# Four K and Q loads issued by ScalarE, and new lists for the first units of a sparse-attention and MLP kernel

## The chip, the cores and the metric

The kernel runs on one core of a Trainium2 chip. The core has five engines that work side by side, each on its own list of instructions: TensorE (PE; its weight loads are shown as PEld), VectorE (DVE), ScalarE (ACT), GpSimd (POOL) and SyncE (SP). In this kernel SP issues DMAs only. The metric is the time of one execution on the device in microseconds (us).

## The reference, cut to what matters

Four batches of eight heads, 768 positions, head size 64. For every query the six best of 24 chunks of 32 keys are chosen by an upper bound from each chunk's smallest and largest key; attention runs over these chunks with a causal mask; the result, with the heads side by side, goes through an MLP with an ELU.

```python
k_min, k_max = k_chunks.min(3), k_chunks.max(3)          # chunks of 32 keys
ub = sum(maximum(q * k_min, q * k_max))                  # per query and chunk
ub = where(causal, ub, -1e9)
top_chunks = argsort(ub)[..., -6:]
scores = where(sel & (pos_q >= pos_k), q @ k.T / 8, -1e9)
x = softmax(scores) @ v                                  # [3072, 512], heads side by side
h = x @ w_in                                             # 512 -> 2048
out = where(h > 0, h, exp(min(h, 0)) - 1) @ w_out        # 2048 -> 512
```

## The kernel before

The work is cut into eight units of 384 query rows. Units 0 and 1 are made of 192 positions each of batches 0 and 1: unit 0 ("p") has positions 0 to 191, where every query takes all of its chunks, and unit 1 ("s") has positions 192 to 383, where chunks are chosen. Units 2 to 7 are half a batch each. For each unit the attention of its rows is followed by an MLP of 16 tiles of 128 hidden channels. Attention of one unit and the MLP of an earlier one are woven into each other.

Names of operations, as the text uses them (b is the batch, u the letter p or s, G a group of four heads, r a pair of heads, x a block of 96 rows):

- `ldk..`, `ldq..`, `ldv..` load K, Q, V into buffers `f` (11 of them, 128 x 512 f32): `ldq1s00` is Q of batch 1, unit s, block 0, and `ldq1s10` block 1. `ec...` copies chunk rows into `lhs`. `wq..` loads Q of unit p on POOL, with a cast to bf16.
- `kT`, `qT` (lines 423 and 408): K and Q are transposed on TensorE into a PSUM bank; `kt`, `qt`, `qh` copy that out, `ka`, `qa` put it into the operands of the score matmuls, `qr` is a relu of Q, `kmin`, `kmax`, `ks` are the chunk bounds.
- `tr` (mask, line 705), `sc` (scores), `ex` (exponential, on ScalarE), `pv` (P times V, line 775), `rcp` and `on` (division, lines 657 and 667 on VectorE or 664 on ScalarE), `px` and `xt` (transposes of the result and their copies).
- `v0p0` and the like convert V to bf16. `ub` (line 613) are the bound matmuls of the choice, `ubT`, `max`, `lt`, `sT`, `mk` make its mask.
- The MLP of unit i: `h0.5` is tile 5 of unit 0 (four matmuls of line 872 into a bank); `e0.5` (ScalarE, exponential), `m0.5` (POOL or VectorE) and `g0.5` (VectorE) make the ELU and free the bank. `o0.1.2` is row tile 1, quarter 2 of the second matrix (line 896).
- `w_in1` (tiles 4 to 7), `w_in0` (0 to 3), `w_in2` (8 to 15) and `w_out0` to `w_out3` load the weights on POOL, with a cast.
- `fill` is a matmul on zeros, 22 of them at the start.

Nothing is scheduled while the kernel runs. A string `ORDER` has three characters for each operation: the engine and the operation's number. A string `PLACES` gives the slot of each buffer (a PSUM bank, an `f` buffer and so on) in order of first use. Each engine works strictly through its own operations in the order of that string; an operation waits until what it reads is there and until the slot that it writes has been left by its earlier buffer's readers.

```python
for j in range(0, len(order), 3):
    o = g.ops[64 * DIGITS.index(order[j + 1]) + DIGITS.index(order[j + 2])]
    for b in o.bufs:
        if b.slot is None and b.cls != "fixed":
            b.slot = DIGITS.index(next(places))
    o.emit({"P": PE, "A": ACT, "D": DVE, "G": POOL, "S": SP}[order[j]])
```

The functions that the change touches:

Of the kernel before, what the change touches and what calls it, by code (L numbers as in the profile page):

```python
# [38 lines left out]
ORDER = """
G0vS0UD00D01PjXA02D09PjYS0sPjZG0wD06Pj-D0iPj+S0uPk0G0aPk1D0oS0rPk2A0TD0jG0kPk3A0tPk4S0XD03G04Pk5  # L40
Pk6Pk7Pk8D05G0bP1mD0lG0cG0WP1hP1nPk9S2dG0eG0pG0VPkaPkbPkcP0KA0OD0PPkdPkeG0nG0gG0fS2fPkfPkgD0qD0m
P18P0RP0IG0dD0SD0MP0BS0zA0JA1cP0+P1iD0CS0xA0FD19P1oP1jS0ZD10D1aD13S2eD0LS2gA1qA1pA15D11GmCP16P1f
P1sS2MA1lGmBD0ND0DD0GS2PS2tP1xA1gD17G0AG08G0yP1wA1kD12P1rP1yS2ND0QP1tA1AGmDP1VA1vA1zD0-P1BP1CP1W
D1DP24P23D25A1uG0YP27P28D26G07D1EG1eP1PP1GD29P1QP1-D1XA2aG0EP1ZD1+D20P1MP1FP1LG2hD1HP2bG1bG2QD1R
P2zD1IA1YP2mD2AP1JD2nP2HP21S2GD1ND1OA1SP1TA2qD2oS2OA1KD22P2uD1UA2cPmYG0HG2sA2ID2BG0hD2pG2CPn4AmZ
Dm-Dm+Pn0An5PmUGn6An1D2vA2JGmEPmQD2wAmVDbqP3jDn7Gn2Dn3A2DS2RAmRGmWPn8A2rG14D3lA1dPmIG2xAn9D3kD3m
GmFA2yPmMD3nPngGnaDmXAmNGmSDnbAmJPnEA2KGmODmTPnsPnAAnhGmGD3oA2FAnFGmKDniPnkD3pGmHDmPA3qA3sPnoDnj
G3rAntP3FDmLAnpGnGPncA3GGnuDnHPnOAnBGnqDnvAndGnCS2kDnrAnlP3+PnwGneA40DnDS2iP3HDnfP36D38A3IP2VD37
P3ZA3tG2LP4jPnIA3-D2XD2WA2ZS4ZPnPA2EG39GnmA2+G2YP4BA3aDnnPnVA4CD41A4kP4DA4EP31P4hP3ePnJA3fD32D33
A4iAnxGnyD4FPnQD34D3gP3uG3JG35DnzG3cG3bPnWA2SD3wS3dA2-D3vD3yD3xA3iS30PnXPnYD3zD2lS2TG2jD3AA3BPnR  # L50
S4-PnKS4YAnSD3ES4XP3LD3CP4MA3hD4lD3DA4NP42DnZP46S4VP3KP43P4GP48A47P4HG2UP4KA49D4IP3QD4JPnLS4WA4L
D3MD3NG4aA3RD4OP3OP4nP4sS7SP4cD44P4bAnMA4tP4mD45P4qA3PD4dD4eP5pP4PP5OS7PA4rG4uD3SP4QD4oP4fP3TA5P
P3UD4RD4SS4+P5dA4gD3VP4TD3WG5RA5qP4wP4vD4pA5eP5CP3XSaLD5QD4xD4yP56A5DS55P5iD57A5aS7QP4zP5HD3YA4A
P5vG7TD4UA5ED58PoHG5gS51Sn-A5mPo3AoID5wA5LPovD5kGoJAo4D5JG59PojA5GG5sD5zA5rPo7Go5DoKAokD5IG5KD5j
PobAowAo8D5xG5lPofA5MGolDo6PoPGo9DomAocA5fS53D7RPoDGodAoQDoaG5yS7UPonA5hGoxDoeAoEGoRPn+SnNDoyAoo
GoFAogScXDoSPozGopA5BDoGPorS8jAo0GohDoqS7LP5TGo1DoiAosA5FDo2S7MGotA5SG5NDouA5tPoLG5bD5VAoAPo+A50
G7VD5UAoMD5XGoBPp0A5oGoNA5cD5WPpcPpdD5YD5ZPp5SnUS5uDoCPp6A5-G5+SaFDoOPpeD61A54DaMP64P6eA65DaOP62
P6aP6gA63Pp1A6bD60A6hDaNP6kP66A6fP6jP68D5nP6cDaPA6lPp7A67G6mD52A6dP6zSaQP6vPoTA69D6iS7KA6AP6tA6w
P6oSnTA6uP6FP6nAoUS7WP6xA6GPoXD6pGoVS7ND6qA6yG5AP6HDoWAoYP6rP6KGbkP6LS7OScPD6sA6IP79GoZP7aP74A6M
P6YDo-PpfA75D6JA7bD6NShDScVG7cDaRP6DA6ZPp2ApgA6EP6BA6CP70P6-P76P6PDp3A6+A77DaSP6ODaTA71P7AP72A73  # L60
P6WA6XP7vP7xA7wA7yDaUP7XD78D6QSb1P6UA6VPp8Ap9P7BSphSp4G7zP8eA8fD7YD7+D6RD7ZP7pP7jP7dP7eP7rP87P7n
D8gA7CG7DD7fD7gD88D89G8iG8hP7tP8wD8xA7kA7qA7oA7sP7lA7mA7uP8kP6SP8DP7EScQSaADb2A8AD8BG8CA6TA8bG8d
P7FD7GD7HA8oP7hA7iP82A83P8rA8sAaGA8tD8mP7ID7JPpiPpCPpOPpqPpKD8yD8pD8cG8aG7-G80SazSaEApDApPDb3D8z
DaWD8lD8EGpEDpFAcWGpQDpRDbmG8nG8qA84A8FDd3ApLDpMDpNPpGPpyApjGpkDplAprP8ID8KD8JScSSaBSaCSpbSaHShF
ApHApzA8HAbnG85GpsG8uD8MDptGpIDpJA81AcYGd0GpADpBPqaAqbPpuPpmApnGpoDppDc+ApvGpwDpxAbpD8LPpSApTDpU
PpWPqeApXGqcD8NA86GpYDpZPq2Pp-Pq6PqiPqjPquPqvD8OScZGc-AbjAaIAq3Ap+Aq7DpVGq0Dq1Dq4Dq5DqdA8PP8TP98
PqkGq8Dq9Ad2AqfGqgDqhSboSaJGaKA8UP99A8GA9aD9bP95A96P8VA8WPqwP8XA8YP91A92P93A94P8ZA8-PqxP8+A90D8R
D8SDaVD8QP9iP9mPakP9wD8vGaXA9jA9xSaDPbxP9uAbyDqyPqlA9vAalD97P9dP9cP9qP9sP9zP9kSfpScRGd5ScTSflSd1
ScUDqmA9nA9tP9AA9BGhID9yD9eD9fA9lA9rP9VA9WPqoD9CPaYP9gD9hP9oA9pP9NPbCA9OP9DPamAanP9PP9-P9EP9+A9Q
# [34 lines left out]
010234561723809400a15670000116732123410154351712367920340512011326120372504022630201740451602060
0001712105100321222310106020041302422105371001210657208104429601a202b10225c63d5074344173e0675174
232002354f0131811a051702149562710202334657702101110353224400271111415003200024301667235013082223
6211124241g0321703025031511642080210211a14023024060172b50d501200217001e9903040645563645270036705
340231510610a143324462420c4518036175460720352160242050221360512703003437015067105025412256406301
2015462720241f034232126300182750369851002011b24115422110702d5117600120301271a12022e1g1502921a044
5364106150341652360311745073a7480420141216521017436560746000200310074351642530340701436007410610  # L110
42322012500347220410676023221c798035120b001246202d1701400505612260110022020f000241743012305621e0
071112221931755412a2640316137544050011601a47135720640203353013120721001117220g041122026531002711
74c02263021d1670105693482300e122f61101154501822304b674310511676271325701101360217051295706272306
123706204523075601020103360271112010022300042411320a621132020237250411ce0252361030170751421bg120
20612350204814010012f010001652733027095310264575302140352735620410026321622347203011031211521200
6712400d341281052302217b02012a13620c211102507243023ef7110g61154420673450256564172631401101225514
60750413270731412054725631203017020025041190221232010711c1006140dg1135221041b7200210711e220f6451
1532608172011
# [51 lines left out]
def kernel(  # L170
# [134 lines left out]
    def dma(dst_src, writes, reads, name, engines=(SP,)):  # L305
        def emit(e):
            d, s_ = dst_src()
            eng[e].dma_start(out=d, in_=s_)
# [693 lines left out]
```

## Time and profile before

| | |
|---|---|
| median of 3 runs | 281.22 us (280.7 to 281.28) |
| profiled execution, its own time | 281.2 us |
| its span, first to last instruction | 279.5 us |
| mean granted TensorE clock | 0.980 |
| busy: PE, DVE, ACT, POOL | 96%, 78%, 78%, 46% of the span |
| DMA | 38.07 MB, mean 136 GB/s; 95,136 of 103,747 packets under 512 B |
| queues | q1 (issued by SP) 32.75 MB, q0 (by POOL) 4.59 MB, q10 (by ACT) 0.30 MB |

The span is cut in tenths and slices on the page; times in the text are microseconds from the span's start. A busy TensorE is not TensorE at its peak: a matmul's time in the groups overlaps its neighbours', so lengths are read from runs of matmuls in the chain. A DMA issue has two times: how long it holds the issuing engine's list, and how long until the data have landed.

### The profile page before, as it was taken

The numbers are of one execution on the slowest core, as the hardware profiler recorded it, in microseconds if no ns is written. First come the engines' busy times: TensorE is split into PE (matmuls) and PEld (weight loads), VectorE is DVE, ScalarE is ACT, GpSimd is POOL, SyncE is SP. The second block draws the span as 40 slices with busy tenths as digits, with TensorE's granted clock in tenths as the row PEclk, the third lists the DMA queues.
The fourth block names the chain that finished last, engine by engine and source line by source line (L and its number), as shares of the span: only waits on it lengthen the run. The fifth ranks groups of instructions, "written<-read, shape, count | busy, mean of one in ns | idle before, by whom it ended". The sixth has DMA issues, their size and how long they took to land.

```text
span 279.5 us, 6962 instructions
## 1 busy us (share of the span) xinstructions
PE 267.7 (96%) x2458; PEld 165.3 (59%) x2458; DVE 217.2 (78%) x655; ACT 217.0 (78%) x491; POOL 128.1 (46%) x256
## 2 busy tenths in 40 slices
...
GB/s 147 211 195 210 224 197 185 216 237 248 53 59 220 233 236 196 211 150 111 192 169 114 116 218 224 69 41 135 164 4 1 58 39 4 14 126 90 20 11 101
DMA packets 103747, 38.07 MB, mean 136 GB/s; under 512 B 95136, under 2 KB 99488, under 8 KB 103712
## 3 DMA queue, kind: packets, MB, share of 16 engines
q1 hardware_dynamic: 95696, 32.75, 55.4%
q0 software_dynamic: 6832, 4.59, 10.9%
q10 hardware_dynamic: 1184, 0.30, 0.5%
...
q14 instruction: 16, 0.13, 0.2%
...
## 4 chain that ended last, share of the span: by engine, by line
PE 75%; DVE 8%; ACT 5%; POOL 2%; issue 2%; DMA 1%; DVEq 0%; ACTq 0%; POOLq 0%
PE bank L896 25%; PE bank L872 24%; PE bank L803 10%; PE bank L854 5%; PE bank L613 3%; PE bank L564 2%; DVE gT L885 2%; ACT pt L818 1%; POOL m L881 1%; PE bank L914 1%; PE bank L690 1%; PE bank L423 1%; ACT e L879 1%; PE bank L775 1%; PE bank L749 1%
## 5 line engine op out<-in xcount | busy, mean ns | idle before, releaser
L872 PE MATMUL bank<-xt,w_in_sb 128*128 128x384 bf16 x512 | 90.2, 328 | 0.3 <-DMA xt<-on 0.2
L896 PE MATMUL bank<-w_out_sb,gT 128*128 128x512 bf16 x368 | 89.3, 379 | 0.0
L881 POOL TENSOR_SCALAR m<-e 128x384 f32<-128x384 f32 x100 | 52.0, 529 | 62.0 <-ACT e L879 51.5
L885 DVE SCALAR_TENSOR_TENSOR gT<-bank,m 128x384 bf16<-128x384 f32 x128 | 65.7, 549 | 9.7 <-POOL m L881 8.4
L879 ACT ACTIVATE e<-bank 128x384 f32<-128x384 f32 x128 | 59.1, 493 | 16.0 <-PE bank L872 13.0
L872 PEld LDWEIGHTS <-w_in_sb 128*128 128x128 bf16 x512 | 49.7, 98 | 35.5 <-issue 4.6
L818 ACT ACTIVATE pt<-bank 128x384 bf16<-128x384 f32 (+1 forms) x144 | 67.1, 547 | 3.6 <-PE bank L803 2.5
L896 PEld LDWEIGHTS <-gT 128*128 128x128 bf16 x368 | 34.6, 97 | 36.1 <-issue 2.2
L803 PE MATMUL bank<-rhs,lhs 96*128 96x384 bf16 (+2 forms) x240 | 42.8, 293 | 1.0 <-DVE on L667 0.5
L835 POOL TENSOR_TENSOR pt<-pt,tri 128x256 bf16<-128x256 bf16 (+1 forms) x18 | 16.4, 916 | 38.5 <-ACT pt L822 23.9
L803 PEld LDWEIGHTS <-lhs 96*128 96x128 bf16 x240 | 21.7, 97 | 13.9 <-issue 0.9
L854 PEld LDWEIGHTS <-pt 128*128 128x128 bf16 x576 | 21.0, 97 | 3.6 <-ACT pt L818 0.2
L854 PE MATMUL bank<-vext,pt 128*128 128x65 bf16 x576 | 22.1, 193 | 0.0
L667 DVE TENSOR_TENSOR on<-bank,rcp 128x384 bf16<-128x384 f32 (+1 forms) x37 | 18.7, 510 | 1.3
L326 POOL CAST rhs<-qt 64x384 bf16<-64x384 f32 x24 | 12.8, 539 | 11.8 <-ACT qt L324 10.8
L324 ACT ACTIVATE o<-bank 128x512 f32<-128x512 f32 (+1 forms) x14 | 8.1, 588 | 13.0 <-PE bank L896 10.1
L657 DVE RECIPROCAL rcp<-bank 128x6 f32<-128x6 f32 (+1 forms) x40 | 7.2, 185 | 13.5 <-PE bank L854 9.0
L371 DVE TENSOR_REDUCE kst<-bank 128x12 f32<-128x384 f32 x32 | 16.5, 548 | 1.3 <-ACT kt L324 0.7
L326 DVE COPY o<-bank 128x512 f32<-128x512 f32 (+1 forms) x11 | 7.2, 665 | 12.2 <-PE bank L896 10.0
L835 DVE TENSOR_TENSOR pt<-pt,tri 128x512 bf16<-128x512 bf16 (+1 forms) x30 | 11.2, 390 | 5.4 <-ACT pt L822 3.6
L324 ACT ACTIVATE rhs<-qt 64x384 bf16<-64x384 f32 x28 | 14.2, 518 | 0.5
L822 ACT ACTIVATE pt<-bank 128x512 bf16<-128x512 f32 x24 | 14.0, 604 | 0.7 <-PE bank L803 0.4
...
## 6 DMA issues: line engine op xcount, KB each, us to landing
...
```

The lines of the kernel that those rows point to most:

```text
L324: nc.scalar.activation(out=dst, in_=src, func=AF.Copy)
L326: eng[e].tensor_copy(out=dst, in_=src)
L667: nc.vector.tensor_tensor(out=ap(on)[:, 0:nt].rearrange("p q h d -> p h q d"), in0=view()[:, :, :, 0:D], in1=ap(rcp)[:, :, 0:nt].to_broadc ...
L803: nc.tensor.matmul(ap(banks[hd])[:, o + pc:o + pc + wd], lhsT=apl(ls, G)[0:96, pr, hd, P * kb:P * (kb + 1)], rhs=ap(rs)[0:96, hd, c0 - HS ...
L818: lambda e, hd=hd, pt=pt, banks=banks, wtot=wtot: nc.scalar.activation(out=ap(pt)[:, hd, PAD:PAD + wtot], in_=ap(banks[hd])[:, 0:wtot], fu ...
L835: eng[e].tensor_tensor(out=view, in0=view, in1=tri[:, 64:64 + P].rearrange("p (a b w) -> p a b w", a=1, b=1) .to_broadcast([P, 2, len(dg), ...
L854: nc.tensor.matmul(view()[:, hd, qi, :], lhsT=ap(pt)[:, hd, P * qi + off:P * qi + off + P], rhs=ap(vx[b])[:, kb, 2 * r + hd, :], start=(kb ...
L872: nc.tensor.matmul(ap(bank)[:, 0:HS], lhsT=w_in_sb[:, kk, P * fc:P * (fc + 1)], rhs=ap(xT[i, kk]), start=(kk == 0), stop=(kk == NKK - 1))
L879: g.op(f"e{i}.{fc}", (ACT,), lambda e, eb=eb, bank=bank: nc.scalar.activation(out=ap(eb), in_=ap(bank)[:, 0:HS], func=AF.Exp), reads=[(ban ...
L881: g.op(f"m{i}.{fc}", (POOL, DVE), lambda e, eb=eb, mb=mb: eng[e].tensor_scalar(out=ap(mb), in0=ap(eb), scalar1=-1.0, scalar2=1.0, op0=AOT. ...
L885: nc.vector.scalar_tensor_tensor(out=ap(gt), in0=ap(bank)[:, 0:HS], scalar=0.0, in1=ap(mb), op0=AOT.max, op1=AOT.min),
L896: nc.tensor.matmul(ap(bank), lhsT=ap(gts[fc])[:, P * tt:P * (tt + 1)], rhs=w_out_sb[:, fc, :], start=(fc == 0), stop=(fc == NFC - 1))
```

## The change

The code changes in one place: the loads of K and Q of batch 1, unit s, may be issued by ScalarE.

```diff
-                            (SP, ACT) if u == 0 and n == "k" else (SP,))
+                            (SP, ACT) if (u, n) == (0, "k") or (b, u) == (1, 1) else (SP,))
```

The rest of the diff is in the two strings. Read back into names, SP's list after its first eleven issues, which are the same, and ScalarE's to the first MLP exponentials:

```diff
 SP
  ... ldk0s10 ldq0s10
- ldk1s00 ldq1s10 ec000 ldk1s10 ec001 ldq1s00 ldv1s0 ldv0s1 ldv0s0 ldq011 ec101 ec100 ldv1s1
+ ec000 ec001 ldv1s0 ldv0s1 ldv0s0 ldq011 ec101 ec100 ldv1s1
  ldq012 ldq010 ldk012 ldk010 ldk011 ldv111 ldq112 ...
 ACT
  table ldk1p00 ldk0p10 kt0p1
- qh0p0 kt1p1 kt0p0 ex0p11 ex0p10 ka11p0 ex0p01 qh1p1 ex0p00 ex1p11 ex1p01 ex1p10 ex1p00
- on1p3 on0p2 on1p1 kt0s0 xtp0 xtp3 qt0s1 e0.4 e0.6 e0.5 qr0s1 e0.3 kt0s1 e0.2 ka00s0 ka01p1
+ ka00p1 ka10p1 qh0p1 ex0p11 kt1p0 ex0p00 ex0p10 ex0p01 qh1p1 qh1p0 ka11p1 ex1p10 ex1p11 ex1p00 ex1p01
+ ka10p0 on0p2 ldk1s00 ldk1s10 on1p1 ldq1s10 xtp0 xtp3 kt0s0 ldq1s00 e0.5 qt0s0 ka01p1 e0.6 e0.4 ka00s0
 DVE
- rcp0p0 rcp0p3 on0p3 on0p0 rcp1p3 rcp0p2 rcp1p2 on1p2 rcp1p0 rcp1p1 on1p0
+ kmax0p0 v0p0 rcp0p3 on0p3 rcp0p0 on0p0 rcp0p2 rcp1p3 on1p3 rcp1p0 rcp1p2 on1p2 on1p0 rcp1p1 rcp0p1
 POOL
- oh es1 es0 w_in1 w_in0 v0p1 tris2 v0p0 w_in2 v1p0 tris1 ka11p1 ks0p0 vc0 ks1p1 vc1 ka10p0 ka10s0 kq ks0s1 m0.6 w_out0
+ oh ks0p1 ka00p0 w_in1 v1p0 es0 w_in0 v0p1 ka01p0 v1p1 w_in2 kq ka11p0 ks0p0 vc1 es1 ka10s0 w_out0 ks0s0 m0.6
 PE (MLP of unit 0 and the scores of unit s)
- h0.4 h0.6 h0.5 h0.3 h0.2 ub00 h0.7 h0.0 h0.1 h0.9 h0.15 h0.12 h0.14 h0.10 h0.11 sc0s00 h0.8 o0.1.0 sc0s11 h0.13 sc0s01 kT1s1 kT1s0 ... o0.0.0 o0.1.1 ... qT1s0 sc0s20 qT1s1
+ h0.5 h0.6 h0.3 h0.2 h0.4 ub00 h0.0 h0.7 h0.1 h0.15 h0.11 h0.9 kT1s1 h0.12 h0.14 h0.8 sc0s10 sc0s00 h0.10 sc0s01 h0.13 kT1s0 o0.0.0 sc0s11 sc0s31 o0.2.0 qT1s1 o0.1.0 sc0s30 o0.1.1 qT1s0
```

Besides, identb goes from VectorE to POOL, the memsets rz and vz0 from POOL to VectorE, v0p0 from POOL to VectorE, on1p3 from ScalarE to VectorE, qt0s0 from VectorE to ScalarE, qt0s1 the other way, and some thirty other small operations of the units p and s change engine or place. Of the 22 fills 18 instead of 14 stand at the very start. The engines' own lists from about 108 us on are the same. The slots of the buffers follow the new order. No operation is added and none is left out.

More of the change, by code (lines that the diff above doesn't have):

```diff
@@ L39 @@
 ORDER = """
[L40 to L66, printed above, removed]
+G0vS0UD00D01PjXA02D09PjYS0sPjZG0wD06Pj-D0iPj+S0uPk0Pk1D0oS0rPk2A0TD0mD0jG08G0aG07G0eG0kPk3A0tPk4
+S0XD03G04G0bG0cPk5Pk6Pk7Pk8Pk9PkaPkbPkcP18PkdPkePkfP0KPkgG05A0OP0BP1iP1mP1nP0RD0pD19D1cA0PD0MD0n
@@ new lines @@
+D1aD0LD0FG0WS2dG0VS2fG0gA0QP0ID0JP0+D10D11D0lP1xA0SP1oP1hP1jS0zA1qA13S0xS0ZA1kD0CD0qD0DG0NG0GS2e
+S2gGmCG0YG0dGmBS2tP1sP1rA1pA1lP1fA1gP16A17P1wP1yA1eA1zP1tA1AA1uA1vG0AD0yP24P23P1MD25P1WP1CD26P1B
+D1DD1EP1VD1XG14G0-P28P27D29P1FP1-P1LP1ZP1GP1PP1QD2aP2bGmDA0HA1YD1HD1+D20A2MP2HP21D1ID1RP2zP1JP2m
+A2NA1SA2PD1ND22D1bD1OP1TD2IP2uD2hD2JD1UA1KA2cPn0A2qA2OS2GD2oAn1Pn4G0hG15D2AD2nD2BA2vD2wDbqA1dPmU
+PmQPmYG0EG2QG0fG2sGmEG2pD2CP3jAn5Gn6Dn7AmZDm-A2rAmRGn2G2LG2xDn3Dm+D3lD3kS2RGmSDmTAmVGmWDmXD3nD3m
+PmIAmJGmKDmLD3oPn8An9GnaPmMAmNA2KGmODmPD3pD2yGmFG12PnEPnoAnpPngA2DAnhDniGmGGmHP36GnqDnbDnrDnjG3r
@@ new lines @@
+A3qAnFGnGDnHPnsAntGnuDnvS2kA2FPnAPncAndP3ZA3-AnBP3FPnkA3GGneD38A3sD2EDnCDnDDnfP3HD3aG3cA3tPnwP2V
+PnIP3+A3IS2iD37A2ZS4ZP4DPnVP3eA40AnlDnmA2-A4EAnxDnnD2XD2WD2YG3bGnyPnOP4BA3fA4CG2SPnPG2+P31D32D3g
+A34P4jP4hA4iA3iPnJA4kA3hPnWPnXD2lD33D39P3uS3dS30PnQPnKDnzPnRAnSD3wD3yD3vD3xD3zD3AD3CA3EA3BS2TPnY
+DnZS4-S4YS4XG41G4FG35G2jP43G3JG4lP3KP4GP4KP48A49P46A47S4VP3LP4MD3MG2UP42D44P4HD45D4IA4NA4LS4WP3Q
+PnLA3RAnMP3OG3DP4qP4sG4aP4bS7SD4OD3ND4JP4cP4QD4dD4eA3PD3SA4rA4tG4uP4nP5pP4PS7PP4mP4fP5OP3UP3TP5d
+A5qA5PG5RD4RD4oD4SP4TS4+A4gP4vP4wP5CP56D3VD3WP3XSaLA5eA4pD5QA5DP5iD4xD4yP4zA4AS55S7QP5HP5vD4UD3Y
@@ new lines @@
+D57G5gA5mA5EPoHAoIS51Sn-Po3A5LA5aPojPovAo4D58G59G7TGoJA5GG5sD5wD5IA5rPo7Go5D5JDoKD5kAokD5jG5KPob
+AowAo8D5xD5zG5lA5MGolDo6PoDPoPGo9DomAocA5fS53D7RGodAoEAoQDoaG5yS7UPofPonA5hGoxDoeGoRPn+SnNDoyAoo
+GoFAogScXDoSGopA5BDoGPorPozS8jAo0GohDoqS7LGo1DoiAosA5FDo2S7MGotA5SDouA5tPoLG5bP5TD5VAoAA50G5NG7V
+D5UAoMD5XGoBPo+Pp0A5oGoNA5cD5WPpcD5YD5ZPp5Pp6SnUS5uDoCA5-G61G5+SaFD52DaMDoOPpdPpeA54P64A65DaOP62
+A63P6gP6aA6bP6ePp1D60A6hDaNP6jP6kP66A6fD5nDaPA6lG6mP68P6cA69A67A6dP6zA6APp7P6vP6tPoTD6iP6oSnTS7K
+S7NSaQA6wP6FP6nA6uAoUS7WP6xA6GPoXD6pD6qA6yG5AP6HGoVDoWAoYP6rP6LP6KGbkS7OScPD6sA6IP79P7aP74A6MP6Y
@@ new lines @@
+GoZDo-PpfA75A7bA6ZD6ND6JShDScVG7cDaRDaTP6DP6BP70P6-Pp2A6EApgA6CP76P6PDp3A6+A77DaSP6OA71P7AP72A73
+P6WA6XP7vA7wP7xA7yDaUP7XD78Sp4Sb1P6UA6VPp8Ap9P7pSphG7zP8eP7BA8fD7YD7+D6QD6RD7ZP7jP7dP7eP7rP7nD8g
+A7CG7DD7fD7gP87D88G8iG8hP7lP8wD8xD89A7kA7sA7qA7oA7mP8kP7tA7uP6SP8DP7EScQSaADb2A8AD8BG8CA6TA8bG8d
+P7FD7GD7HA8oP7hA7iP82A83P8rA8sAaGA8tD8mP7ID7JPpiPpCPpOPpqPpKD8yD8pD8cG8aG7-G80SazShFApDApPDb3D8z
+DaWD8lD8EGpEDpFGpQDpRDbmG8nG8qA84AcWA8FDd3ApLDpMDpNPpGPpyApjGpkDplAprP8IScSSaBSpbSaCSaHApHApzG85
+D8KD8JSaEA8HAbnGpsD8MDptGpIG8uDpJA81AcYGd0GpADpBPqaAqbPpuPpmApnGpoDppDc+ApvGpwDpxA86AbpD8LPpSApT
@@ L67 @@
+DpUPpWPqeApXD8NGpYGqcDpZPq2Pp-Pq6PqiPqjPquPqvD8OScZGc-AbjAaIAq3Ap+Aq7DpVGq0Dq1Dq4Dq5DqdA8PP8TP98
 PqkGq8Dq9Ad2AqfGqgDqhSboSaJGaKA8UP99A8GA9aD9bP95A96P8VA8WPqwP8XA8YP91A92P93A94P8ZA8-PqxP8+A90D8R
@@ L74 @@
 AbvPrgPbMDbNGqWDqXDbOArhAhHProAdaGrmDrnDbPGriDrjGg6DbQPr0PqMPqAGbKArpAbBGrqDrrAr1Gr2AqNGqOAdoAqB
-PqQAqRGqSAf+DbRDr3DbSDqPPddAdePrwArxPdiAdjPqYAqZGqCDqDDftDqTGbTGryPr4PrsAbVAr5DbWGq-Dq+DfvPrAPbZ
-AdfArtAbUPbXAbYAb-PrGGr6Dr7DrzPcbPrHPc9Pc0PcfAccAg3GruGdgGb+DrvDfuDdpAcaPc1Ac2PctPceAcgPcsPcDAcu
-GchPcGPcHPcpAcqPrIPcnPcBPrJDc3DcdPc4Pc5AcIDcJSqzSfhShwSfwDfxSg1PcjPrMPciPrBAcoGcrDc6Dc7ShxSqnSc8
+PqQAqRGqSAf+DbRDr3DbSDqPPddAdePrwArxPdiAdjPqYAqZGqCDqDGbTGryPr4SqzSfhShwDftDqTPrsAbVAr5DbWGq-Dq+
+DfvPrAPbZAdfArtAbUPbXAbYAb-PrGGr6Dr7DrzPcbPrHPc9Pc0PcfAccAg3GruGdgGb+DrvDfuDdpAcaPc1Ac2PctPceAcg
+PcsPcDAcuGchPcGPcHPcpAcqPrIPcnPcBPrJDc3DcdPc4Pc5AcIDcJSfwDfxSg1PcjPrMPciPrBAcoGcrDc6Dc7ShxSqnSc8
 AcCAcEGcFDcvDckDclScmPcwPcxDcyDczPrCScAGhNDfyPcKPcLDcMDcNScOAdmAdhAdkPdsPrDAg5ArKAdrAdqAdlGhEGhL
@@ L103 @@
 PLACES = """
[L104 to L118, printed above, removed]
+0102345612034567001012789a0012102034011317612033123540100112302672531005032216260704370305614490
+0110765231002112011202032240001504105226032062117278920a012b451044226510cd3304250131371260e05126
@@ new lines @@
+3224773316f00111811a5740560163121012622173572062332490517404101340456230010021117202531141428723
+301102262g02211034114031210535706130220a102621172282950d01400101725003e60a6504124066402110762417
+002026322200b016243441001c1458106214610620527243010207433030234061063157012037425045121416003101
+6041036701222f031234015521262714965011012019104327026400811d1027311010524671a01220e2g1120a12b032
+4550403112504313692542701275a7152310123023464217055132703000301311270511302120360721053027020310
+22301012102147120001376203612c6980310419224103600d0702401501341072201016200f00230072522211203312
@@ new lines @@
+e0271042601a54714121b25005134371060014312a47235700601103315002210714201117101g000226213154210602
+70c20253212d0370424693456510e210f3101141052281032693745421027736745617222013326472140a4703276323
+403723105165171601022105332670221042012300001211511b320232262037111002ce20515301322627100029g410
+62300511124840020200f1200017127532670a1512634175520241356751610420216211302307103012050011112621
+3701022d342084011516207900222b45311c010221126605103ef7402g32110412375051057130476654012101261540
+307120232707514462107656540030171100112002a2610051120702c4213002dg123160014297122241602e101f3010
@@ L119 @@
+2551718271042
 """
```

## The prediction

> **What bounds the kernel now.** I read the page first, then the chain of waits in order of time, then the stretches of one microsecond for the opening, then the timeline of the stretch that the change touches, last the DMA queues.
>
> ```profile
> span 279.5 us, 6962 instructions
> PE 267.7 (96%) x2458; PEld 165.3 (59%) x2458; DVE 217.2 (78%) x655; ACT 217.0 (78%) x491; POOL 128.1 (46%) x256
> ```
>
> ```profile
> 60.48 8.44 PE bank L872 x50
> ...
> 255.23 9.10 PE bank L872 x56
> ```
>
> TensorE is the bound. In the chain (second fence: start, length, what), from about 60 us to the end, one run of matmuls follows another; 50 matmuls of line 872 in 8.44 us are 0.169 us each, and 56 in 9.10 us, at the far end, 0.163. The engines' own lists are the same from about 108 us on. So what the change does before that is passed on whole: the end moves by as much as TensorE gets ahead or behind in the opening.
>
> ```profile
> 11.00:12.00 1.00, 0.05 (x1) 0.06 (x2) 1.00 (x3) 0.61 (x3) 0.74 (x8) 1.00 1.11 201
> 12.00:13.00 1.00, 0.90 (x9) 0.60 (x10) 1.00 (x4) 1.00 (x3) 0.82 (x5) 0.65 1.24 202
> 13.00:14.00 1.00, 1.00 (x4) 0.29 (x2) 1.00 (x5) 0.88 (x2) 1.00 (x3) 0.50 1.39 184
> 15.00:16.00 1.00, 0.54 (x10) 0.38 (x7) 0.58 (x1) 0.84 (x2) 0.93 (x4) 0.64 1.33 203
> 20.00:21.00 1.00, 1.00 (x8) 1.00 (x9) 0.58 (x4) 0.60 (x3) 0.80 (x4) 0.50 1.24 200
> ```
>
> The columns are length, busy time of PE, PEld, DVE, ACT and POOL, granted clock, DMA share and GB/s. After the idle microsecond at 11 (TensorE busy for 0.05) the clock falls to 0.50 within the microsecond at 12 (mean 0.65, so at about 12.3) and is back within that at 15 (mean 0.64, at about 15.7): a period of 3.4 us. At 20 us it stands at 0.50 again. A new idle stretch there is paid twice: as itself, and as matmuls at half speed behind it.
>
> **The change, first part: TensorE reaches the first MLP block earlier.** Rows of the timeline (start, length, engine, line, operation, and in brackets the idle time before it and its releaser):
>
> ```profile
> 16.86 0.71 PE L775 MATMUL bank<-vext,pt 128*128 128x65 bf16 x18 [1.32 <-POOL vext L337]
> ...
> 18.27 1.14 PE L775 MATMUL bank<-vext,pt 128*128 128x65 bf16 x30 [0.70 <-POOL vext L337]
> ...
> 18.94 0.93 ACT L664 ACTIVATE on<-bank,rcp 128x64 bf16<-128x64 f32 x4 [1.71 <-DVE rcp L657]
> ...
> 19.92 0.39 PE L690 MATMUL bank<-ident_b,on 128*128 128x128 bf16 x2 [0.30 <-ACT on L664]
> ...
> 20.19 0.42 DVE L667 TENSOR_TENSOR on<-bank,rcp 128x256 bf16<-128x256 f32 x1
> ...
> 23.02 0.90 ACT L324 ACTIVATE xt<-bank 128x384 bf16<-128x384 bf16 x2
> ```
>
> The P·V products wait for POOL's V conversions at 16.86 and 18.27, the transposes for ScalarE's division at 19.92. The new lists put v0p0 on VectorE and v1p0 ahead of the weight loads, and on1p3 on VectorE (0.42 us for ScalarE's 0.93). That lets the second group of P·V start about 17.0 instead of 18.27 (-1.3) and takes 0.5 off the division: -1.8 together. ScalarE then still has on0p2 (0.93), two DMA issues, on1p1 (0.93), a third issue, and the copies xtp0 and xtp3 (0.90). From 17.5, with a wait of about 0.4 for the reciprocal and 0.55 for each issue (row below), 17.5 + 0.93 + 1.1 + 0.4 + 0.93 + 0.55 + 0.9 is 22.3. So the first MLP block, which begins at 23.95, begins at about 22.1 by the first sum and 22.3 by the second; I take 22.1.
>
> **Second part: ScalarE stands in a DMA issue.** Four loads (K and Q of batch 1's second unit) leave SP's list. On ScalarE two stand behind on0p2, ldq1s10 behind on1p1, and ldq1s00 directly ahead of e0.5, the first exponential of the MLP. An issue is cheap only while its queue has room:
>
> ```profile
> 0.81 2.02 SPq L308 DMA_DIRECT2D f<-in_k_dram  x4
> 2.87 0.48 SPq L308 DMA_DIRECT2D f<-in_v_dram  x1
> 3.40 1.10 SPq L308 DMA_DIRECT2D f<-in_k_dram  x1
> ...
> 16.09 0.55 SPq L308 DMA_DIRECT2D f<-in_k_dram  x1
> ...
> 18.13 4.26 SPq L308 DMA_DIRECT2D f<-in_q_dram  x1
> 22.48 4.64 SPq L308 DMA_DIRECT2D f<-in_v_dram  x1
> ```
>
> ```profile
> q1 hardware_dynamic: 795, 0.20, 25.7%
> ```
>
> ```profile
> q0 software_dynamic: 1232, 1.72, 95.4%
> q1 hardware_dynamic: 1072, 0.33, 21.7%
> ```
>
> The second fence is SP's queue q1 from 0 to 3.4 us, the third the queues from 18 to 28 us. A load of 96 rows by 8 heads is 768 packets of 256 B. By 3.4 us SP had issued 768 + 3 x 384 + 1,024 = 2,944 data packets and 795 had moved; with some 2,150 outstanding the issues, 0.5 us until then, grew to 1.10 us. From 18 to 28 us the weight queue q0 and q1 send nearly packet for packet, and q1 moves only 1,072 in 10 us, 107 per us. The very load that is moved, ldq1s00, held SP 4.26 us there.
>
> ScalarE's queue starts empty. From about 18.3 us it takes three loads, 2,304 packets; by 22.4 it has moved about 4.1 x 107 = 440, which leaves 1,860. The fourth makes 2,630, and 2,150 fit with little slack; draining 480 to 600 (the completion packets counted in) at 107 per us takes 4.5 to 5.6 us, and a third queue among the same engines can only slow that. I take 5.6. The ends: 0.55 if the queue has room (row at 16.09), and 7.0 by the row at 22.48, where a load of 512 packets took 4.64 us (x 768/512). It is nearest to the row of 4.26, which is the same load in the same stretch.
>
> The Trainium skill, "DMA: Bandwidth & Descriptors", section "Issuing engines are not separate DMA queues", says that issuing from several engines only saves the sequencer's time of initiating, usually small beside the DMA itself. The 4.26 us row disagrees with "small" here. By the rule the sum would be the faster rival below.
>
> Behind the blocked issue stand, in ScalarE's order, e0.5, qt0s0, ka01p1, e0.6, e0.4 and all later exponentials. What TensorE has meanwhile:
>
> ```profile
> 23.95 4.42 PE L872 MATMUL bank<-xt,w_in_sb 128*128 128x384 bf16 x20
> 28.29 0.56 PE L613 MATMUL bank<-qt,kst 64*32 64x192 f32 x16
> ...
> 29.11 6.02 PE L872 MATMUL bank<-xt,w_in_sb 128*128 128x384 bf16 x36
> ...
> 37.80 0.96 PE L423 MATMUL bank<-ident_f,f 96*128 96x96 f32 x8
> ...
> 39.04 1.89 PE L896 MATMUL bank<-w_out_sb,gT 128*128 128x512 bf16 x8
> ...
> 41.55 0.39 PE L749 MATMUL bank<-rhs,lhs 96*128 96x128 bf16 x3 [0.62 <-ACT lhs L324]
> ...
> 42.87 0.49 PE L423 MATMUL bank<-ident_f,f 96*128 96x96 f32 x4
> ```
>
> ```profile
> 27.46 0.36 DVE L348 TENSOR_SCALAR qr<-qt 128x384 f32<-128x384 f32 x1
> ```
>
> ```profile
> L881 POOL TENSOR_SCALAR m<-e 128x384 f32<-128x384 f32 x100 | 52.0, 529 | 62.0 <-ACT e L879 51.5
> L885 DVE SCALAR_TENSOR_TENSOR gT<-bank,m 128x384 bf16<-128x384 f32 x128 | 65.7, 549 | 9.7 <-POOL m L881 8.4
> L879 ACT ACTIVATE e<-bank 128x384 f32<-128x384 f32 x128 | 59.1, 493 | 16.0 <-PE bank L872 13.0
> ```
>
> Five MLP tiles (20 matmuls, at 0.163 us 3.3 us) run without ScalarE: to 25.4. The next, ub00, needs qt0s0, which moved from VectorE to ScalarE behind e0.5, and its relu. With the issue from 22.4 to 28.0: e0.5 to 28.5, qt0s0 (about 0.5, as the copies above) to 29.0, relu 0.36 to 29.4, ub00 at 29.4 against 28.29. After it h0.0 needs the bank of h0.6: ka01p1 to 29.5, e0.6 to 30.0, m0.6 0.53, g0.6 0.55, so 31.1; the corresponding tile stood at 29.11. That is +2.0, the 1.8 us of the first part spent already. TensorE idles from 25.4 to 29.4, longer than the stretch that halved its clock at 13 us. One such period, 3.4 us at half speed, loses 1.7: +1.7. The wait of 0.62 us at 41.55 goes, since ScalarE can catch up: -0.6.
>
> **Third part: the rest.** The removed issues free SP's queue, but SP's next ones are chunk rows and V loads that TensorE needs only after 50 us: nothing. POOL loses two memsets to VectorE and gains identb; its weight loads start within about 1 us of before, hidden by the wait above. The changed places of buffers and the reordered score matmuls I cost at nothing: they run where TensorE is fed already.
>
> The sum: 2.0 + 1.7 - 0.6 = +3.1 us. The profiled execution took 281.2 us, 1.7 more than its span, and the median of the runs shown is 281.22, so both bases agree: 284.3 us.
>
> **Rivals.** *The loads land too late (slower).* If ScalarE's queue takes the fourth load at once, TensorE runs on and meets kT1s1, moved forward, and qT1s1 instead. Rows of landing (last column, us after issue), from 16 to 28 us:
>
> ```profile
> f<-in_k_dram SPq DMA_DIRECT2D x1, 192.0 KB, 14.7
> f<-in_q_dram SPq DMA_DIRECT2D x1, 192.0 KB, 14.3
> ```
>
> There 16.09 + 14.7 is 30.8 and 18.13 + 14.3 is 32.4, well ahead of the users at 37.80 and 42.87. In the new list, ScalarE's 3,072 packets at 107 to 130 per us from 18.3 end at 42 to 47. Without its delay qT1s1, two groups of 0.94 us and a small one earlier than 42.87, stands at about 40.9 counted from before. That gives +1 to +6, in the middle +3.7: 284.9. Against it: gaps in the weight queue would speed the loads up.
>
> The same page's section "Queues, rings and completion order" has each engine take turns between queues by packets. The 1,232 against 1,072 packets agree; it favours this rival only if the issue itself does not block.
>
> *Faster.* The fourth issue takes at most about 2 us, since the exponentials before had 1.2 us of idle in front, and the weight queue pauses so that the loads land by 40. Then the 1.8 us stay, and the five tiles, 4.34 us from 23.95 to 28.29 by their rows, take 3.3 at full clock: -0.9 or so. 281.2 - 2.7 = 278.5. For it: ScalarE's queue is empty at 18.3. Against it: the count above.
>
> *Not what it says.* The four loads are issued no sooner than SP did (18.13 for the last, against about 22.4); only what stood behind them on SP gains, which nobody waits for. If block and gain then cancel, the time is 281.2.
>
> **How the numbers follow.** Blocked issue 0.55, late landing 0.20, faster 0.20, cancelled 0.05. The likeliest alone reaches from 281.5 (issue of 4.5, no clock loss: 281.2 + 0.9 - 0.6) to 288.0 (issue of 7.0, two clock periods, the wait of 0.62 kept: 281.2 + 3.4 + 3.4). The range reaches down into the faster case, 279.4, and up to 288.0; outside lie about half of the faster case and a tenth of the slower ones. A measurement of this kernel tells 0.2% from no change, 0.56 us. Faster 0.20, the same 0.05, slower 0.75.
>
> **What would show it.** Right: an ACTq row of 4 to 7 us in front of the first exponential near 22 us, TensorE idle near 26 to 29, a clock of 0.5 near 29 to 33, later rows alike with a shift of about 3 us. Wrong: ScalarE's four issues at 0.5 us each; then an idle stretch before kT1s1 or qT1s1 released by a DMA is the second case, and its absence, with the first MLP block near 22 us, the faster one.

## The result, and the profile after

The changed kernel takes 288.2 us (median of four runs, 287.97 to 289.43) against 281.25 us of the kernel before, measured beside it: ratio 1.0261 with a 95% interval of 1.0239 to 1.0283, +7.0 us. The forecast was 284.3 us, +3.1; the sign is right, the size too small, and 288.2 lies just above the range's end of 288.0. The profiled execution took 289.43 us, the slowest of the four: 8.2 more than that of before, 1.2 more than the medians differ. Times are medians; one of the four runs of e_sp_qt0late, at 287.77 us against 282.91 to 284.28, fell in a slower state and is left out.

The page of the changed kernel: span, granted clock in 40 slices, and the chain by engine and by line. Below it the chain by engine of the kernel before.

```profile
span 287.7 us, 6965 instructions
...
PEclk9977799999999999999999999999999999999999
...
PE 67%; DVE 13%; POOL 7%; DMA 5%; issue 4%; ACT 3%; ACTq 0%; POOLq 0%; DVEq 0%
PE bank L896 23%; PE bank L872 22%; PE bank L803 8%; DMA f<-in_k_dram 5%; PE bank L854 4%; PE bank L613 3%; DVE gT L885 2%; PE bank L564 2%; DVE kst L371 2%; POOL m L881 2%; ACT e L879 2%; DVE on L667 1%; PE bank L914 1%; PE bank L775 1%; DVE kn L514 1%
```

```profile
PE 75%; DVE 8%; ACT 5%; POOL 2%; issue 2%; DMA 1%; DVEq 0%; ACTq 0%; POOLq 0%
```

DMA had 1% of the chain and has 5%, under the line "f<-in_k_dram". The chain between 15 and 36 us (start, length, what) shows where:

```profile
17.61 0.03 ACT on L664
...
17.67 12.98 DMA f<-in_k_dram
...
30.72 0.32 ACTq L308
...
31.14 0.49 ACT e L879
31.64 0.38 ACT qt L324
32.02 0.40 ACT lhs L324
32.41 0.38 ACT e L879
...
32.88 0.52 POOL m L881
...
33.42 0.57 DVE gT L885
...
34.03 2.08 PE bank L872 x6
```

The piece of 12.98 us is the load of a K block, issued at 17.67 and landed at 30.65. What it releases is not a reader of K but ScalarE's next DMA issue, ldq1s00 (line 308, 0.32 us). Then come the first exponential, qt0s0, ka01p1, e0.6, m0.6, g0.6 and h0.0: exactly the sequence of the prediction's second part, with another cause ahead of it and later. ScalarE's timeline:

```profile
17.67 0.32 ACTq L308 DMA_DIRECT2D f<-in_k_dram  x1
...
18.11 0.49 ACTq L308 DMA_DIRECT2D f<-in_k_dram  x1
...
23.46 1.45 ACTq L308 DMA_DIRECT2D f<-in_q_dram  x1
...
24.96 0.87 ACT L324 ACTIVATE xt<-bank 128x384 bf16<-128x384 bf16 x2 [0.84 <-PE bank L423]
25.72 0.50 ACT L324 ACTIVATE kt<-bank 128x384 bf16<-128x384 f32 x1
30.72 0.32 ACTq L308 DMA_DIRECT2D f<-in_q_dram  x1
31.14 0.49 ACT L879 ACTIVATE e<-bank 128x384 f32<-128x384 f32 x1 [4.93 <-DMA f<-in_k_dram]
```

The fourth issue, forecast as a row of 5.6 us, is a row of 0.32 us; the 4.5 us from 26.2 to 30.7 lie in front of it, as a wait. TensorE meanwhile (line 423 transposes Q of unit s as well as K; the row at 22.27 is qT0s1):

```profile
15.73 2.66 PE L775 MATMUL bank<-vext,pt 128*128 128x65 bf16 x46 [0.24 <-POOL vext L337]
...
22.27 0.48 PE L423 MATMUL bank<-ident_f,f 96*128 96x96 f32 x3 [3.29 <-DMA f<-in_q_dram]
...
25.73 3.57 PE L872 MATMUL bank<-xt,w_in_sb 128*128 128x384 bf16 x20
32.07 0.56 PE L613 MATMUL bank<-qt,kst 64*32 64x192 f32 x16 [2.77 <-ACT qt L324]
...
34.03 2.39 PE L872 MATMUL bank<-xt,w_in_sb 128*128 128x384 bf16 x7 [0.61 <-DVE gT L885]
```

P·V ends at 18.4 (15.73 + 2.66), a microsecond sooner than before (18.27 + 1.14 = 19.4), but the first MLP block starts at 25.73, not at 23.95 as before or at 22.1 as forecast. ub00 comes at 32.07 (before 28.29) and the tile behind it at 34.03 (before 29.11): +4.9 us here.

More is added later. First row: the MLP of unit 1 in the kernel before; second and third: the same block in the changed one; fourth: a score matmul of batch 0 in the changed one. Then VectorE's waits from 60 to 72 us in the changed kernel (total, times, longest), and the last MLP block in its chain.

```profile
59.98 8.94 PE L872 MATMUL bank<-xt,w_in_sb 128*128 128x384 bf16 x52
```

```profile
66.34 3.56 PE L872 MATMUL bank<-xt,w_in_sb 128*128 128x384 bf16 x20
70.48 6.46 PE L872 MATMUL bank<-xt,w_in_sb 128*128 128x384 bf16 x36 [0.58 <-DVE kst L371]
...
86.21 0.38 PE L803 MATMUL bank<-rhs,lhs 96*128 96x384 bf16 x2 [0.95 <-DVE gT L885]
```

```profile
DVE kst L371 <- ACT kt L324: 2.3, 1, 2.3
```

```profile
263.46 9.10 PE bank L872 x56
```

The block that began at 59.98 begins at 66.34, +6.4; the one at 255.23 (shown in the prediction) at 263.46, +8.2. So 1.4 us more are lost between 34 and 66 us, and 1.9 after that; the two stops shown, which the kernel before doesn't have, are 1.5 us long together (0.58 + 0.95).

### The profile page after: what moved, and what is told of

It is laid out like the page before. It is cut to its first block, busy times and chain, and to the rows that moved or that the text cites. A ratio compares the mean times of both kernels' runs of the same rounds, so it can differ in the third digit from the quotient of the medians.

```text
span 287.7 us, 6965 instructions
## 1 busy us (share of the span) xinstructions
PE 269.5 (94%) x2458; PEld 166.3 (58%) x2458; DVE 219.8 (76%) x654; ACT 216.6 (75%) x490; POOL 131.5 (46%) x258
## 4 chain that ended last, share of the span: by engine, by line
PE 67%; DVE 13%; POOL 7%; DMA 5%; issue 4%; ACT 3%; ACTq 0%; POOLq 0%; DVEq 0%
PE bank L896 23%; PE bank L872 22%; PE bank L803 8%; DMA f<-in_k_dram 5%; PE bank L854 4%; PE bank L613 3%; DVE gT L885 2%; PE bank L564 2%; DVE kst L371 2%; POOL m L881 2%; ACT e L879 2%; DVE on L667 1%; PE bank L914 1%; PE bank L775 1%; DVE kn L514 1%
## 5 line engine op out<-in xcount | busy, mean ns | idle before, releaser
L854 PE MATMUL bank<-vext,pt 128*128 128x65 bf16 x576 | 22.1, 193 | 0.0
```

The costliest lines, as they stand in the source:

```text
L854: nc.tensor.matmul(view()[:, hd, qi, :], lhsT=ap(pt)[:, hd, P * qi + off:P * qi + off + P], rhs=ap(vx[b])[:, kb, 2 * r + hd, :], start=(kb ...
```

## The experiments

Two theories for ScalarE's stand. **A, a counter:** in the built program the loads of SyncE and ScalarE count their landing on eight completion counters in turn, and a load waits until the load before it on its counter, the eighth ahead in the sequence of both engines, has landed; for ldq1s00 that is ldk1s00. The trace of the changed kernel bears this out: these loads name eight semaphores (108, 111 and 113 to 118), ldk1s00 and ldq1s00 name the same one, 111, and ScalarE's wait for 111 ends at 30.69, after the landing at 30.65. **B, room:** ScalarE's own DMA queue is full, as predicted. Beside them **C:** the new lists cost the time by themselves.

**The loads on ScalarE alone, in the lists of before (b_loads_act).**

```diff
 SP  ... ldq0s10
- ldk1s00 ldq1s10 ec000 ldk1s10 ec001 ldq1s00 ldv1s0
+ ec000 ec001 ldv1s0
 ACT
- ... on0p2 on1p1 ... e0.4
+ ... on0p2 ldk1s00 ldk1s10 on1p1 ldq1s10 ... ldq1s00 e0.4
```

> The kernel before, with all of its lists, and only the four loads of batch 1's second unit moved to ScalarE at places like the changed kernel's (both K loads behind on0p2, ldq1s10 behind on1p1, ldq1s00 before e0.4). If the loads on ScalarE cost by themselves what they seem to cost in the changed kernel (a stand of ScalarE in front of ldq1s00 until ldk1s00 has landed, about 30 to 31 us), the first MLP block stops for about 3 to 4 us and the time is 284 to 286 us. If the cost comes from the rearranged lists, 281 to 282 us.

287.86 us, ratio 1.0237 [1.019, 1.0283]: the loads alone cost as much as the whole change, more than expected. ScalarE's timeline, and the row of TensorE's first MLP block:

```profile
21.83 5.00 ACTq L308 DMA_DIRECT2D f<-in_q_dram  x1
...
31.32 0.32 ACTq L308 DMA_DIRECT2D f<-in_q_dram  x1
31.74 1.26 ACT L879 ACTIVATE e<-bank 128x384 f32<-128x384 f32 x3 [3.22 <-DMA f<-in_k_dram]
```

```profile
28.11 5.26 PE L872 MATMUL bank<-xt,w_in_sb 128*128 128x384 bf16 x20 [4.52 <-DVE kst L371]
```

There are two stands, of two kinds: 5.00 us in the issue of the third load, ldq1s10, and 3.2 us in front of the fourth until a K load has landed.

**Only the two K loads on ScalarE, lists of before (b_kloads_act).**

```diff
 SP  ... ldq0s10
- ldk1s00 ldq1s10 ec000 ldk1s10 ec001 ldq1s00
+ ldq1s10 ec000 ec001 ldq1s00
 ACT
- ... on0p2 on1p1
+ ... on0p2 ldk1s00 ldk1s10 on1p1
```

> The kernel before, with only the two K loads on ScalarE behind on0p2; the Q loads stay on SyncE. All four on ScalarE gave 287.9 in these lists. If the third and fourth load are what ScalarE is held by (5.0 us in the issue of ldq1s10, 3.2 us in front of ldq1s00), nothing is held: 280.5 to 282.5 us. If any load on ScalarE in this stretch costs, 284 us or more.

282.46 us, ratio 1.0046 [1.0032, 1.006]. ScalarE isn't held. What is left is 1.5 us by the medians; the trace has a wait of TensorE for an output weight, which the kernel before doesn't have:

```profile
37.22 1.02 PE L896 MATMUL bank<-w_out_sb,gT 128*128 128x512 bf16 x4 [1.18 <-DMA w_out_sb<-in_moe_w_out_dram]
```

The third and fourth load thus cost 5.4 us of the 7.0.

**Which load is waited for (e_split_v).** The changed kernel; one load of V between ldk1s00 and ldq1s00 is issued as two halves, so that every later load falls one counter further.

```diff
+            if name == "ldv0s0":
+                for h in range(2):
+                    eng[e].dma_start(out=d[:, 4 * h:4 * h + 4], in_=s_[:, 4 * h:4 * h + 4])
+                return
             eng[e].dma_start(out=d, in_=s_)
```

> The changed kernel; only SyncE's load ldv0s0, which stands between ldk1s00 and ldq1s00 in the sequence of loads, is issued in two halves (same bytes, one DMA more). Theory A (each load of SyncE and ScalarE waits for the landing of the eighth load ahead of it): ldq1s00 now has ldv0s1 eight ahead of it instead of ldk1s00; that one landed at 33.6 in the changed kernel, ldk1s00 at 30.65. ScalarE is held until about 33 to 34 instead of 30.7, ub00 at about 35, 290 to 291.5 us. Theory B (only room in ScalarE's own queue): ScalarE's queue carries the same, held until 30.7 as before, 287.8 to 288.7 us.

291.09 us, ratio 1.0353 [1.032, 1.0386].

```profile
22.26 3.30 ACTq L312 DMA_DIRECT2D f<-in_q_dram  x1
25.61 0.87 ACT L328 ACTIVATE xt<-bank 128x384 bf16<-128x384 bf16 x2 [4.38 <-issue]
...
32.33 0.32 ACTq L312 DMA_DIRECT2D f<-in_q_dram  x1
32.75 0.49 ACT L883 ACTIVATE e<-bank 128x384 f32<-128x384 f32 x1 [5.88 <-DMA f<-in_v_dram]
```

The releaser is now a load of V, which ScalarE neither reads nor issued, and the time rises by 2.9 us (by the medians) for the same bytes. The releaser is what theory A names, and not B, for the stand in front of the fourth load. The third load is held in its issue, 3.30 us, as B has it. Before that, about one of the 4.38 us in which ScalarE does nothing is a counter too: that of the third load is ec001's here, which lands at 22.19.

**All four at once (e_four_early).**

```diff
 ACT
- on0p2 ldk1s00 ldk1s10 on1p1 ldq1s10 xtp0 xtp3 kt0s0 ldq1s00 e0.5
+ on0p2 ldk1s00 ldk1s10 ldq1s10 ldq1s00 on1p1 xtp0 xtp3 kt0s0 e0.5
```

> The changed kernel, with all four loads on ScalarE right behind one another, at the place of the first (17.7 us); nothing else is moved. Theory A (a load waits for the landing of the one eight ahead of it): the counters of the last two are now those of ldq0s10 (landed 22.2) and ec001 (landed 24.9), so ScalarE stands from 18.6 to 22.2 and to about 24.9, where it had nothing to do until 23.2 anyway, and not after that: e0.5 at about 28.3, ub00 at about 29.3, 285.4 us (284 to 287), faster than the changed kernel. Theory B (room in ScalarE's queue): the fourth load finds three ahead of it and stands until the first is away, about 30.7, with on1p1 and the whole projection behind it: ub00 at 36, 291.5 to 293.5 us, slower than the changed kernel.

290.22 us, ratio 1.0325 [1.0303, 1.0346].

```profile
18.01 1.61 ACTq L308 DMA_DIRECT2D f<-in_k_dram  x1
...
19.71 7.54 ACTq L308 DMA_DIRECT2D f<-in_q_dram  x2
27.35 0.93 ACT L664 ACTIVATE on<-bank,rcp 128x64 bf16<-128x64 f32 x4 [8.94 <-issue]
```

The counters were those of loads that had landed early, and ScalarE was held all the same: 7.54 us in two issues, until 27.25. A alone (284 to 287) is refuted; B's order, slower than the changed kernel, came, though its forecast (291.5 to 293.5) was a little high. Both mechanisms exist, and which one binds depends on where the load stands.

**The fourth load later (e_q00_late).**

```diff
 ACT
- kt0s0 ldq1s00 e0.5 ... e0.0 e0.7 e0.1
+ kt0s0 e0.5 ... e0.0 e0.7 ldq1s00 e0.1
```

> The changed kernel, with only ScalarE's ldq1s00 moved from ahead of the first exponential to behind the eighth (e0.7). Theory A: seven more loads of SyncE have been counted by then, and the load eight ahead is now ldv0s0 (landed 36.8 in the changed kernel): the first exponential comes at about 26.3 and ub00 at about 28.3, but ScalarE then stands from about 30 to about 35 to 37 behind e0.7; 287 to 291 us. Theory B: by 30 us its own queue has room again (ldk1s00 lands at 30.65), no stand over 1 us, 283.5 to 285 us.

286.97 us, ratio 1.0216 [1.0173, 1.0259].

```profile
20.67 4.38 ACTq L308 DMA_DIRECT2D f<-in_q_dram  x1
25.09 0.87 ACT L324 ACTIVATE xt<-bank 128x384 bf16<-128x384 bf16 x2 [4.49 <-issue]
...
33.11 0.32 ACTq L308 DMA_DIRECT2D f<-in_q_dram  x1
```

No stand at 33.11: by the trace's packets ldv0s0 had landed at about 32.4, sooner than A's forecast took it to, and just before ScalarE came there. B's time is missed too, since the third issue (4.38 us) holds the first block until 25.6. The run doesn't tell the theories apart. It shows that the wait in front of the fourth load, taken away, is worth only 1.2 us while the third issue stands.

**The wait at qT0s1 (e_qt0late).**

```diff
 PE
- pxp3 qT0s1 pxp2 kT0s1 pxp0 kT0s0 pxp1 qT0s0
+ pxp3 pxp2 kT0s1 pxp0 kT0s0 pxp1 qT0s1 qT0s0
```

> The changed kernel, with only TensorE's qT0s1 moved behind pxp1, so that nothing of the norm and projection waits behind ldq0s10's landing. First MLP block at about 22 to 22.5 us instead of 25.73. Theories A and B (the stand of ScalarE in front of ldq1s00 sets the end, the 3.3 us lies beside it): ldq1s00 is issued at 30.7 as before, ub00 at 32, 287.2 to 288.5 us. Theory C (the 3.3 us adds to the end by itself): 285 us.

288.53 us, ratio 1.0276 [1.0258, 1.0294]: no gain. ScalarE comes to its third issue sooner and stands in it longer, and the first MLP block starts where it did:

```profile
21.03 4.27 ACTq L308 DMA_DIRECT2D f<-in_q_dram  x1
25.35 0.87 ACT L324 ACTIVATE xt<-bank 128x384 bf16<-128x384 bf16 x2 [4.60 <-issue]
```

```profile
25.89 5.47 PE L872 MATMUL bank<-xt,w_in_sb 128*128 128x384 bf16 x20 [4.04 <-ACT xt L324]
```

The third issue ends at 24.91 in the changed kernel and at 25.30, 25.56 and 25.05 in e_qt0late, e_split_v and e_q00_late, whenever it began (23.46, 21.03, 22.26, 20.67). The 3.3 us at qT0s1 lie beside that.

These ends go with what ScalarE's queue q10 has moved by then, as the DMA view of the same traces counts it. In the changed kernel q10 moves no packet until 21.5, 3.8 us after the first load was issued, 70 by 22.4 and 283 by 24.91, the end of the third issue. In e_qt0late, e_split_v, e_q00_late, e_four_early and b_loads_act it has moved 278, 305, 259, 260 and 205 when the third issue ends. In e_two_moves (below) the third issue begins only at 25.11, with 296 moved, and takes 0.32 us. The four loads are 3,136 packets, so three are 2,352 and some 2,050 to 2,150 of them were left each time. It isn't a fixed number: the fourth issue of e_four_early ends at 27.25, with 448 of 3,136 moved. SyncE's issues stand in the same stretch (5.30 us from 21.61 in b_loads_act), so it isn't shown whether the room is ScalarE's own.

**The new lists with the loads on SyncE (e_sp, e_sp_qt0late, e_qloads_sp).**

```diff
 SP (e_sp, e_sp_qt0late)
+ ldq0s10 ldk1s00 ldq1s10 ec000 ldk1s10 ec001 ldq1s00 ldv1s0
 SP (e_qloads_sp; the K loads stay on ACT)
+ ldq0s10 ec000 ldq1s10 ec001 ldq1s00 ldv1s0
 PE (e_sp_qt0late)
+ pxp3 pxp2 kT0s1 pxp0 kT0s0 pxp1 qT0s1 qT0s0
```

> The changed kernel's lists, with only the four loads of batch 1's second unit back on SyncE at the places they had before. In the changed kernel ScalarE stands from 26.2 to 30.7 us in front of the load ldq1s00. Whether it stands there for a completion counter (theory A: each load waits for the landing of the load eight ahead of it, here ldk1s00, landed 30.65) or for room in its own queue (theory B, the prediction's), the stand goes with the loads: e0.5 at about 26.6, ub00 at about 28, and about 4 us off: 284 us (282.5 to 285.5). If the rearranged lists cost most of the 7 us by themselves (theory C: the transposition qT0s1 waits 3.3 us for the load ldq0s10, which shares the DMA engines with weight loads that are issued sooner), the time stays at 286.5 or more.

> Both edits of the two runs beside it: the four loads on SyncE and qT0s1 behind pxp1. If the two waits are the whole of it, 280.5 to 282.5 us (before: 281.2): the 3.3 us counts once ScalarE's stand is gone. If 283.5 or more is left, some third part of the lists costs over 2 us (the weight loads w_out1 to w_out3, later by 6 to 8 us, or the clock).

> The changed kernel, with only the two Q loads of that unit back on SyncE; the two K loads stay on ScalarE behind on0p2. ScalarE then has two loads where the changed kernel had four: no stand in front of ldq1s00, by the counter (theory A) and by room (theory B) alike; e0.5 at 24 to 27 us. Against e_sp (285.5), where kT1s1 waits 2.0 us for a K load that is issued later from SyncE, this wait should go: 283 to 285 us. If it stays at 288, the stand of ScalarE is not what costs the time.

285.5 us (1.0158 [1.0117, 1.02]), 283.3 us (1.0092 [1.0065, 1.012]) and 285.47 us (1.0163 [1.0108, 1.0218]). Taking the loads, or the Q loads alone, off ScalarE is worth 2.7 us, not the 4 expected, and the new lists still cost 4.5 without them. With qT0s1 moved as well another 2.2 go, and 2.3 are left over the kernel before; the forecast for that run, if the two waits were the whole, was 280.5 to 282.5. e_qloads_sp misses its 283 to 285: its profile has no wait at kT1s1, but qT0s1 waits 4.83 us for ldq0s10. TensorE's timeline in e_sp shows why the early start isn't kept:

```profile
22.76 4.14 PE L872 MATMUL bank<-xt,w_in_sb 128*128 128x384 bf16 x20
...
34.13 0.47 PE L423 MATMUL bank<-ident_f,f 96*128 96x96 f32 x3 [1.85 <-DMA f<-in_k_dram]
```

The first MLP block does start 1.2 us sooner than before. But kT1s1, which the new lists moved forward, comes before its K.

**The two later stops (e_two_moves).**

```diff
 ACT
- kt011 qr012 e1.11 kt013 kt010 e1.1
+ kt010 kt011 qr012 e1.11 kt013 e1.1
 DVE
- g1.9 v011 kminc200a g1.12
+ g1.9 g1.12 v011 kminc200a
```

> The changed kernel, with two single moves in the lists of batch 0's second pair of units: ScalarE's kt010 ahead of kt011 (in the changed kernel it is copied at 67.94, last of three, and VectorE's kmax010 waits 2.27 us for it, then TensorE's h1.2 0.74 us for the bank), and VectorE's g1.12 right behind g1.9 (TensorE's sc01020 waits 1.11 us for it). TensorE falls behind the kernel before by 2.3 us more between 59 and 97 us in the changed kernel. If these two stalls are that loss: 286 to 286.8 us, 1.5 to 2.2 off. If the slack is taken elsewhere, 288.

286.87 us, ratio 1.0209 [1.0165, 1.0254]: 1.3 us off by the medians, less than expected, and the interval overlaps that of the changed kernel. TensorE's two stops at lines 872 and 803 are gone from its waits between 55 and 110 us; the longest left is

```profile
PE bank L854 <- DVE pt L835: 0.6, 1, 0.6
```

**All repairs, and then kT1s1 later (e_qsp_moves_qt0, e_repairs_kt1_late).** The first is e_qloads_sp with e_qt0late's and e_two_moves' edits; the second adds

```diff
 PE
- h0.9 kT1s1 h0.12 h0.14 h0.8 sc0s10 sc0s00 h0.10 sc0s01
+ h0.9 h0.12 h0.14 h0.8 sc0s10 sc0s00 h0.10 kT1s1 sc0s01
```

> All repairs together: the Q loads on SyncE, the two list moves, and TensorE's qT0s1 behind pxp1. If the costs are the stand of ScalarE (about 3 to 4), the two stalls (about 2) and the 3.3 us at qT0s1 (worth about 1.7 once ScalarE is free, from e_sp against e_sp_qt0late), nearly all of the 7 us is gone: 280 to 282 us. At 283 or more, a further cost is left, most likely TensorE's half-speed periods, which the changed lists move from the attention of the first unit into the first MLP block.

> The kernel of e_qsp_moves_qt0 (284.2), with TensorE's kT1s1 moved behind h0.10, to about the place among the MLP tiles that it had in the kernel before. In e_qsp_moves_qt0 kT1s1 waits 2.7 us (31.9 to 34.8) for a K load of batch 1. If the transfers of the start set the pace, the wait at kT1s1 goes, and 1.5 to 2.5 us with it: 281.5 to 283 us. If the next operation that needs those loads or the MLP weights waits as long, 284 us.

284.23 us (1.0105 [1.0061, 1.0148]), above the 280 to 282 expected, then 280.43 us (0.9979 [0.9963, 0.9995]). TensorE in the first, then in the second:

```profile
34.83 0.47 PE L423 MATMUL bank<-ident_f,f 96*128 96x96 f32 x3 [2.66 <-DMA f<-in_k_dram]
```

```profile
29.75 4.08 PE L872 MATMUL bank<-xt,w_in_sb 128*128 128x384 bf16 x24 [0.69 <-DMA w_in_sb<-in_moe_w_in_dram]
34.24 0.60 PE L749 MATMUL bank<-rhs,lhs 96*128 96x128 bf16 x6 [0.42 <-DVE gT L885]
```

With kT1s1 back where its K has landed, 3.8 us go, more than its wait of 2.66, and the kernel is as fast as before or a little faster: 0.2%, with the interval just below 1. The further cost was thus kT1s1 ahead of its K, and not the half-speed periods that the expectation thought most likely. In this last kernel the K loads are still issued by ScalarE, the Q loads by SyncE.

## Why the prediction was too low

**First part, TensorE at the first MLP block at 22.1: failed.** P·V gained its microsecond. The sum then gave each of ScalarE's issues 0.55 us. Two took 0.32 and 0.49, but the third, ldq1s10, is held by room, and behind it stand xtp0 and xtp3. In the profiled execution on1p1, and with it the third issue, came only at 23.20 and 23.46, since TensorE stood 3.29 us at qT0s1 for ldq0s10, a wait that the sum didn't have; then the issue took 1.45 us, and the first block came at 25.73. Without that wait (e_qt0late) the issue takes 4.27 and the block comes at 25.89, so either is enough. The step that failed is the speed of ScalarE's queue: 440 packets were counted as moved by 22.4, at 107 per us from 18.3, and 70 had moved. With so few the prediction's own limit, about 2,150 packets, would have held the third load, which it let pass, and 2,050 to 2,150 were left when that load's issue ended.

**Second part, ScalarE held in the issue of ldq1s00: right place, wrong cause, wrong size.** The stretch was forecast as 22.4 to 28.0; it was 26.2 to 30.7, 4.5 us instead of 5.6, as a wait for the landing of ldk1s00 (e_split_v) and not as an issue. The working behind it held operation by operation: from the end of the issue to ub00 1.4 us were forecast (28.0 to 29.4) and 1.0 measured (31.04 to 32.07), to h0.0 3.1 forecast and 3.0 measured. So the +2.0 was mis-sized by the time of the release alone: h0.0 at 34.03 against 29.11 is +4.9.

**The clock: the period came, but not as an added one.** One period of half speed was forecast near 29 to 33 for +1.7. In the changed kernel the microsecond at 33 has a granted clock of 0.50, those at 34 and 35 too, and the one at 36 ends it:

```profile
33.00:34.00 1.00, 0.41 (x12) 0.11 (x1) 0.58 (x2) 0.95 (x3) 0.93 (x3) 0.50 1.22 198
36.00:37.00 1.00, 1.00 (x7) 0.57 (x6) 0.95 (x7) 0.37 (x2) 0.62 (x2) 0.86 1.16 227
```

From 34.03 to 66.34 TensorE lost 1.4 us against the kernel before (+4.9 to +6.4). The first 2.3 us of that stretch, to 36.3, ran at half speed, which by estimate from these rows costs 1.1. But the mean granted clock from 10 to 37 us is 0.81 in both kernels: before, the first MLP block ran in part at half speed (0.52 in the microsecond at 25) and took 4.42 us, in the changed kernel 3.57. So the sum counted the new period and not the one that went.

**The wait of 0.62 us that should go, -0.6: failed.** In the changed kernel a wait of 0.67 us stands at the same line, 749, at 42.13, with another releaser (DVE gT), and the shift only grows.

**The rest at nothing: failed, by 1.9 us.** Reordered lists past 60 us were passed over because TensorE "is fed already". Two operations, kt010 and g1.12, had gone further back in their engines' lists, and TensorE came to wait for them. e_two_moves, which moves them forward, got 1.3 us back.

**The rivals.** "The loads land too late" didn't happen in the changed kernel, since ScalarE's stand came first, but it stands right behind: with the stand away, kT1s1 waits 1.85 us in e_sp and 2.66 in e_qsp_moves_qt0. The fourth issue was short, as the faster rival has it (0.32 us), but with 4.5 us of waiting in front of it, for which neither the prediction nor a rival had a term. The lists alone (e_sp, +4.5) and the loads alone (b_loads_act, +7.0) don't add up to 11.5 but to 7.0, so each must hide part of the other.

**The rules cited.** The Trainium skill, "DMA: Bandwidth & Descriptors", section "Issuing engines are not separate DMA queues", calls what an issue costs its sequencer usually small relative to the DMA itself. Two loads on ScalarE agree (0.32 and 0.49 us in the changed kernel), the third doesn't (5.00 in b_loads_act). The Trainium skill, "DMA: Bandwidth & Descriptors", section "Why a DMA increments its semaphore by 16 and not by 1", says that a wait can pass too early when two DMAs in flight share a semaphore. No run here shows that; it may be the reason for the wait on the counter, whose price e_split_v shows.

**Open:** why ScalarE's queue moves its first packet only 3.8 us after the first issue; whether the room that its third issue waits for is its own; why the landing of ldq0s10 differs so much (TensorE waits 3.29 us for it in the changed kernel, 0.68 in e_split_v, not at all in e_q00_late, with the same lists up to there); and what each edit in e_repairs_kt1_late is worth alone.
